# Linear attention and a gated feed-forward: kv products as half-height matmuls on alternating row halves

## The chip, the cores and the metric

The kernel runs on one core of a Trainium2 chip. A core has a matrix engine (TensorE, PE in the profile), three engines for elementwise work (VectorE or DVE, ScalarE or ACT, GpSimd or POOL), a SyncE queue that issues most transfers (SP), and 16 DMA engines. The metric is the device time of one execution in microseconds, the median of several; lower is better.

## What is computed

```python
def _attn_ref(q, k, v):                       # q, k, v: (8, 8, 576, 64), f32
    def phi(x):
        return np.where(x > 0, x, np.exp(x) - 1.0) + 1.0
    q_p, k_p = (phi(q), phi(k))
    kv = np.einsum('bhsd,bhse->bhde', k_p, v)
    z = np.sum(k_p, axis=2)
    num = np.einsum('bhsd,bhde->bhse', q_p, kv)
    den = np.einsum('bhsd,bhd->bhs', q_p, z)[..., None] + 1e-06
    return num / den

def _moe_ref(x, w1, w2, w3, w_out):           # x: (4608, 512); w1, w2: (512, 1024)
    a = x @ w1                                # w3: (1024, 1024); w_out: (1024, 512)
    b_ = x @ w2
    h = a * b_ @ w3
    return h @ w_out
```

The attention is linear: for each of 64 batch-head pairs, kv is a 64x64 product over the sequence of 576, and z is a sum of phi(k). The result, as 4608 tokens of 512 features, goes through two projections, their product, and two more matrices. The kernel multiplies w3 by w_out once (w_f) and uses that.

## The kernel before

A token batch b has 576 = 4 x 128 + 64 positions: four full chunks ("J") and a rest of 64 ("R"). The rests of heads 0 to 3 lie on partitions 0 to 63 and those of heads 4 to 7 on partitions 64 to 127. The body is one long list of short steps in a fixed order, the string ORDER; the letter is the step, then batch (or token chunk) and part. L, M, N load k, q, v; E, C, B load the weights w3, w_out, w1 and w2; x, y, z (for k) and X, Y, Z (for q) are the exp, min and max of phi; v casts v; K makes kv; A is the numerator and denominator; T and a, b transpose q; P and D transpose the result; F is one f block of the two projections; O is one output block, S its store, Q the last one; w, U, W make w_f; c, d, e, f, g and h, i serve the first batch. A "+" after a step moves its copy from ScalarE to VectorE (or a load of a rest from SyncE's queue to GpSimd's).

The pools. A tile of at_ps is two PSUM banks, of mm_ps one:

```python
    ld = ctx.enter_context(tc.tile_pool(name="ld", bufs=5))       # raw q, k, v and w3 blocks
    lr = ctx.enter_context(tc.tile_pool(name="lr", bufs=2))
    sm = ctx.enter_context(tc.tile_pool(name="sm", bufs=3))
    mm_ps = ctx.enter_context(tc.tile_pool(name="mm_ps", bufs=4, space=bass.MemoryType.PSUM))
    at_ps = ctx.enter_context(tc.tile_pool(name="at_ps", bufs=2, space=bass.MemoryType.PSUM))
```

The kv step, K. A pair of heads (hp) makes one 128x130 product: 128 features of two heads by twice 64 values and a column of ones, which gives z. Four matmuls contract over 128 positions and one over the 64 of the rest, all into one bank. A step does two pairs, and one copy takes the result to SBUF:

```python
    def kv_full(b, g):


        kj, kr = ph["k", b]
        if g == 0:
            kvs[b] = att.tile([P, KC, 2, D + 1], BF16, tag="kv", name="kv")
        kvp = at_ps.tile([P, 2, 512], F32, tag="at", name="kvp")
        W = 2 * (D + 1)
        rows = slice(g * R, (g + 1) * R)
        for i in range(2):
            hp = 2 * g + i
            for j in range(NJ):
                nc.tensor.matmul(kvp[:, 0, i * W:(i + 1) * W],
                                 kj[:, hp, j].rearrange("p u d -> p (u d)"),
                                 vt[:, j, 2 * hp:2 * hp + 2, :].rearrange("p h e -> p (h e)"),
                                 start=(j == 0), stop=False)
            nc.tensor.matmul(kvp[:, 0, i * W:(i + 1) * W], kr[rows, i * P:(i + 1) * P],
                             vr[rows, 2 * i:2 * i + 2, :].rearrange("p h e -> p (h e)"),
                             start=False, stop=True)
        return kvp[:, 0, 0:2 * W]

    def kv_copy(b, g, p, alt=False):
        copy_of(alt)(out=kvs[b][:, 2 * g:2 * g + 2].rearrange("p a u e -> p (a u e)"), in_=p)
```

The step A, which reads kv. Each matmul contracts over the 64 features of one head, so it uses one row half of the array (u = 0 or 1) and writes the bank of that half; a full chunk has stationary tiles of 64x128, the rest of 64x64:

```python
            ... (cut)
            nd = at_ps.tile([P, 2, 512], F32, tag="at", name="nd")
            if j == 0:
                xns[b] = att.tile([P, NJ, H, D], BF16, tag="xn", name="xn")
            if j < NJ:
                n, dst = P, xns[b][:, j]
            else:
                n = R
                dst = xns[b, "R"] = att.tile([R, H, D], BF16, tag="xnr", name="xnr")
            for hp in range(KC):
                if j < NJ:
                    w = qts[b, 0][:, hp, j * P:(j + 1) * P]
                else:
                    hh, i = divmod(hp, 2)
                    w = qts[b, 1][:, i, hh * R:(hh + 1) * R]
                for u in range(2):
                    rows = slice(u * D, (u + 1) * D)
                    nc.tensor.matmul(nd[0:n, u, hp * (D + 1):(hp + 1) * (D + 1)], w[rows],
                                     kvs[b][rows, hp, u, :], start=True, stop=True)
            v4 = nd[0:n, :, 0:KC * (D + 1)].rearrange("p u (c e) -> p u c e", e=D + 1)
            r = lr.tile([P, 2, KC], F32, tag="r", name="r", bufs=4)
            work.append((n, dst, v4, r))
        for n, dst, v4, r in work:
            nc.vector.tensor_scalar_add(out=r[0:n], in0=v4[:, :, :, D], scalar1=1e-6)
        for n, dst, v4, r in work:
            nc.vector.reciprocal(out=r[0:n], in_=r[0:n])
        for n, dst, v4, r in work:
            nc.vector.tensor_tensor(
                out=dst.rearrange("p (c u) e -> p u c e", u=2), in0=v4[:, :, :, 0:D],
                in1=r[0:n].unsqueeze(3).to_broadcast([n, 2, KC, D]), op=ALU.mult)
```

The step F (two times four matmuls of 512 columns, a ScalarE copy and a VectorE product) and the step O (eight matmuls of 512 columns and a copy):

```python
    def f_open(c, f):
        if f == 0:
            abs_[c] = ab_p.tile([P, FC, NCH], BF16, tag="ab", name="ab")
        return [mm_ps.tile([P, NCH], F32, tag="mm", name=n) for n in ("a_ps", "b_ps")]

    def f_mm(c, f, ps, w, kc):
        nc.tensor.matmul(ps, w[:, kc, f * P:(f + 1) * P], xt[:, 4 * c:4 * c + 4, kc, :],
                         start=(kc == 0), stop=(kc == KC - 1))

    def f_close(c, f, a_ps, b_ps):
        a_sb = sm.tile([P, NCH], F32, tag="a_sb", name="a_sb")
        nc.scalar.copy(out=a_sb, in_=a_ps)
        nc.vector.tensor_mul(out=abs_[c][:, f, :], in0=a_sb, in1=b_ps)

    def f_unit(c, f):
        a_ps, b_ps = f_open(c, f)
        for ps, w in ((a_ps, w1_sb), (b_ps, w2_sb)):
            for kc in range(KC):
                f_mm(c, f, ps, w, kc)
        f_close(c, f, a_ps, b_ps)

    def o_unit(c, m, alt=False):
        ab = abs_[c]
        o_ps = mm_ps.tile([P, DM], F32, tag="mm", name="o_ps")
        for f in range(FC):
            nc.tensor.matmul(o_ps, ab[:, f, m * P:(m + 1) * P], wf_sb[:, f, :],
                             start=(f == 0), stop=(f == FC - 1))
        o_sb = o_sbs[c, m] = sm.tile([P, DM], F32, tag="o_sb", name="o_sb", bufs=OBUF)
        copy_of(alt)(out=o_sb, in_=o_ps)
```

The w3 blocks share the pool ld with q, k and v; four blocks make one tile, and each block is transposed on TensorE:

```python
    def load_w3(i):
        if i % 4 == 0:
            t = ld.tile([P, JW], F32, tag="ld", name="w3b")
            w3s[i // 4] = t.bitcast(BF16).rearrange("p (i n) -> p i n", i=4)
        t = raw["w3", i] = w3s[i // 4][:, i % 4]
        return nc.gpsimd.dma_start(out=t, in_=moe_w3[i * P:(i + 1) * P, :])

    def w3_tr(i, alt=False):
        t = w3ts[i] = setup.tile([P, FC, P], BF16, tag="w3t", name="w3t", bufs=3)
        tp = at_ps.tile([P, FC, P], BF16, tag="at", name="w3p")
        for kc in range(FC):
            nc.tensor.transpose(tp[:, kc, :], raw["w3", i][:, kc * P:(kc + 1) * P], ident)
        copy_of(alt)(out=t, in_=tp)
```

Of the kernel before, what the change touches and what calls it, by code (L numbers as in the profile page):

```python
# [18 lines left out]
def kernel(  # L19
# [11 lines left out]
    nc = tc.nc  # L31
    B, H, S, D = q.shape
# [28 lines left out]
    att = ctx.enter_context(tc.tile_pool(name="att", bufs=2))  # L61
    lr = ctx.enter_context(tc.tile_pool(name="lr", bufs=2))
# [3 lines left out]
    at_ps = ctx.enter_context(tc.tile_pool(name="at_ps", bufs=2, space=bass.MemoryType.PSUM))  # L66
# [12 lines left out]
    vt = wpool.tile([P, NJ, H, D + 1], BF16)  # L79
    vr = wpool.tile([P, H // 2, D + 1], BF16)  # L80
# [44 lines left out]
    ph = {}  # L125
# [39 lines left out]
    def copy_of(alt):  # L165
        return nc.vector.tensor_copy if alt else nc.scalar.copy
# [309 lines left out]
    GATES = "E4<M0.1 L0.0<E0 L1.2<E3 M0.0<E0 M1.2<C1 N1.0<E7"
    ctx.enter_context(tc.manual_schedule())
# [13 lines left out]
    def step(s):  # L491

        alt = s.endswith("+")
        op, *at = s.rstrip("+").replace(".", " ").split()
        b = int(op[1:]) if op[1:] else None
        i = int(at[0]) if at else None
        t = op[0]
        if t == "F":
            f_unit(b, i)
        elif t == "O":  # L500
            o_unit(b, i, alt)
        elif t == "S":
            o_store(b, i)
        elif t == "Q":
            o_last(b, i)
        elif t == "I":
            constants(b)
        elif t == "H":
            warm_up(b)
        elif t == "w":  # L510
            w3_tr(b, alt)
        elif t == "U":
            wf_mm(b, 0)
            held["U", b] = True
# [87 lines left out]
```

## Time and profile before

| | |
|---|---|
| median of 3 runs | 264.65 us (264.34 to 265.21) |
| span of the profiled run | 263.7 us |
| matmuls, weight loads | 1544, 1561 in the records (some matmul records are missing) |
| TensorE clock granted | 1.0 throughout |
| HBM | 38.80 MB read, 9.44 MB written |

The page gives busy time per engine; "PEld" is the loading of stationary operands, which overlaps the matmuls. Digits in the rows of slices are tenths of a slice (1/40 of the span, 6.6 us). A line of the waits reads: engine and source line, the engine and line that released it, total us, number of times, longest. In the lists of instructions, 128*128 or 64*128 after a matmul is rows*columns of its stationary operand, and 128x130 is partitions x columns of the moving one. Times of matmuls overlap, as they are pipelined, so the distance between starts tells what one costs.

By group (total busy us, mean ns of one): the F matmuls 75.1 and 74.9 (380, 379), the O matmuls 63.2 (379), kv full height 12.7 (222), kv rest 7.3 (227), A 5.9 and 2.2 (192, 197). The copy of kv is ten times on ScalarE (3.7 us, 374 ns) and four times on VectorE (1.7 us, 427 ns).

### The profile page before, as it was taken

The page shows a single profiled execution, that of the slowest core. Times are in us where ns is not written, and L with a number is a line of the kernel's source. Part 1 is how long each engine was busy: PE and PEld are TensorE (multiplying, and loading weights), DVE is VectorE, ACT ScalarE, POOL GpSimd, SP SyncE. Part 2 cuts the span into 40 slices and gives each one's busy share as a digit, 9 for nine tenths or more (in the row PEclk, how much of TensorE's full clock was granted, in tenths as well). Part 3 has the DMA queues.
Part 4 walks back from the last instruction along what each step waited for, and adds up shares of the span by engine and source line. Part 5 has one row for each costly group of instructions (what it writes and reads, how often), then busy time and mean ns, then how long its engine had stood idle before and what let it go on. Part 6 is the DMA issues. An engine that isn't in the chain of part 4 may idle for free.

```text
span 263.7 us, 4270 instructions
## 1 busy us (share of the span) xinstructions
PE 241.5 (92%) x1544; PEld 118.5 (45%) x1561; DVE 167.9 (64%) x421; ACT 125.0 (47%) x196; POOL 20.1 (8%) x40
## 2 busy tenths in 40 slices
PE   1149999899999999999999999999999999999993
PEld 1125454445454455455444444454445444444442
DVE  0037688769976978999867389557974744324330
ACT  1048576856858663677244454545432212331411
POOL 8001754000100001000000000000000000000000
PEclk9999999999999999999999999999999999999999
DMA  6999999999798398959959996923871063002024
GB/s 88 215 257 368 311 231 235 221 339 283 266 300 226 43 318 221 311 137 266 217 112 245 265 286 124 277 70 108 233 199 42 9 136 106 0 22 98 2 80 160
DMA packets 70564, 48.97 MB, mean 186 GB/s; under 512 B 34928, under 2 KB 64880, under 8 KB 70544
## 3 DMA queue, kind: packets, MB, share of 16 engines
q1 hardware_dynamic: 63648, 42.67, 59.4%
q0 software_dynamic: 6752, 5.90, 13.7%
q8 instruction: 12, 0.20, 0.3%
q10 hardware_dynamic: 144, 0.13, 0.1%
q14 instruction: 8, 0.07, 0.1%
HBM read 38.80 MB, written 9.44 MB: 183 GB/s over the span
## 4 chain that ended last, share of the span: by engine, by line
PE 81%; DMA 13%; SPq 2%; ACT 1%; issue 1%; DVE 0%; POOL 0%; POOLq 0%
PE a_ps L345 24%; PE b_ps L345 23%; PE o_ps L364 23%; DMA w3b<-in_moe_w_dram 5%; DMA k<-in_k_dram 4%; DMA v<-in_v_dram 4%; PE kvp L193 3%; PE nd L239 3%; PE kvp L197 2%; SPq L111 1%; PE wf_ps L438 1%; PE tp L283 1%; PE xtp L259 1%; PE o_ps L391 1%; PE w3p L428 1%
## 5 line engine op out<-in xcount | busy, mean ns | idle before, releaser
L345 PEld LDWEIGHTS <-w_sb 128*128 128x128 bf16 x576 | 54.2, 98 | 62.5
L351 DVE TENSOR_TENSOR ab<-a_sb,b_ps 128x512 bf16<-128x512 f32 x72 | 49.2, 685 | 51.5 <-PE b_ps L345 40.4
L345 PE MATMUL a_ps<-xt,w_sb 128*128 128x512 bf16 x288 | 75.1, 380 | 0.0
L345 PE MATMUL b_ps<-xt,w_sb 128*128 128x512 bf16 x288 | 74.9, 379 | 0.0
L350 ACT COPY a_sb<-a_ps 128x512 f32<-128x512 f32 x72 | 42.0, 585 | 60.9 <-PE a_ps L345 59.8
L364 PE MATMUL o_ps<-wf_sb,ab 128*128 128x512 bf16 x266 | 63.2, 379 | 0.7
L364 PEld LDWEIGHTS <-ab 128*128 128x128 bf16 x280 | 26.7, 98 | 30.8 <-DVE ab L351 0.2
L367 ACT COPY o_sb<-o_ps 128x512 f32<-128x512 f32 x21 | 12.2, 583 | 35.0 <-PE o_ps L364 35.0
L162 DVE SCALAR_TENSOR_TENSOR kj<-k,e 128x256 bf16<-128x256 f32 x64 | 23.7, 417 | 0.1
L162 DVE SCALAR_TENSOR_TENSOR qj<-q,e 128x256 bf16<-128x256 f32 x64 | 23.4, 417 | 0.2
L137 ACT ACTIVATE e<-q 128x1024 bf16<-128x1024 f32 x16 | 16.7, 1058 | 13.2 <-DMA q<-in_q_dram 13.0
L428 PE MATMUL w3p<-ident,w3b 128*128 128x128 bf16 x64 | 6.2, 253 | 15.8 <-DMA w3b<-in_moe_w_dram 8.0
L137 ACT ACTIVATE e<-k 128x1024 bf16<-128x1024 f32 x16 | 16.9, 1055 | 3.8 <-DMA k<-in_k_dram 2.4
L249 DVE TENSOR_TENSOR xn<-nd,r 128x512 bf16<-128x512 f32 x28 | 18.0, 686 | 0.0
L438 PE MATMUL wf_ps<-wo_sb,w3t 128*128 128x512 bf16 x61 | 16.8, 414 | 0.7 <-ACT w3t L429 0.5
L367 DVE COPY o_sb<-o_ps 128x512 f32<-128x512 f32 x14 | 9.6, 688 | 10.6 <-PE o_ps L364 10.6
L141 DVE TENSOR_SCALAR er<-er 128x256 bf16<-128x256 bf16 x16 | 3.5, 220 | 17.4 <-ACT er L137 17.4
L141 DVE TENSOR_SCALAR e<-e 128x1024 bf16<-128x1024 bf16 x32 | 13.5, 421 | 0.3 <-ACT e L137 0.3
L193 PE MATMUL kvp<-vt,kj 128*128 128x130 bf16 x128 | 12.7, 222 | 0.9 <-ACT vt L171 0.9
L428 PEld LDWEIGHTS <-w3b 128*128 128x128 bf16 x64 | 4.9, 114 | 17.5 <-DMA w3b<-in_moe_w_dram 9.3
L193 PEld LDWEIGHTS <-kj 128*128 128x128 bf16 x128 | 8.3, 98 | 5.3 <-issue 1.3
L171 ACT CAST vt<-v 128x1024 bf16<-128x1024 f32 x9 | 9.4, 1046 | 0.9 <-DMA v<-in_v_dram 0.9
(77 smaller groups left out, 155.7 us busy)
## 6 DMA issues: line engine op xcount, KB each, us to landing
out_dram<-o_sb SPq DMA_DIRECT2D x31, 256.0 KB, 3.2
k<-in_k_dram SPq DMA_DIRECT2D x7, 1024.0 KB, 8.0
q<-in_q_dram SPq DMA_DIRECT2D x7, 1024.0 KB, 7.4
v<-in_v_dram SPq DMA_DIRECT2D x6, 1024.0 KB, 5.9
w3b<-in_moe_w_dram POOLq DMA_DIRECT2D x8, 256.0 KB, 7.6
v<-in_v_dram SPq DMA_DIRECT2D x4, 512.0 KB, 9.1
w_sb<-in_moe_w_dram POOLq DMA_DIRECT2D x8, 256.0 KB, 11.5
out_dram<-o_sb SPq DMA_DIRECT2D x9, 128.0 KB, 2.5
```

The lines of the kernel that those rows point to most:

```text
L137: nc.scalar.activation(out=e, in_=x, func=AF.Exp)
L141: nc.vector.tensor_scalar_min(out=e, in0=e, scalar1=1.0)
L162: nc.vector.scalar_tensor_tensor(out=out, in0=x, scalar=1.0, in1=e, op0=ALU.add, op1=ALU.max)
L193: nc.tensor.matmul(kvp[:, 0, i * W:(i + 1) * W], kj[:, hp, j].rearrange("p u d -> p (u d)"), vt[:, j, 2 * hp:2 * hp + 2, :].rearrange("p h ...
L249: nc.vector.tensor_tensor(out=dst.rearrange("p (c u) e -> p u c e", u=2), in0=v4[:, :, :, 0:D], in1=r[0:n].unsqueeze(3).to_broadcast([n, 2 ...
L345: nc.tensor.matmul(ps, w[:, kc, f * P:(f + 1) * P], xt[:, 4 * c:4 * c + 4, kc, :], start=(kc == 0), stop=(kc == KC - 1))
L350: nc.scalar.copy(out=a_sb, in_=a_ps)
L351: nc.vector.tensor_mul(out=abs_[c][:, f, :], in0=a_sb, in1=b_ps)
L364: nc.tensor.matmul(o_ps, ab[:, f, m * P:(m + 1) * P], wf_sb[:, f, :], start=(f == 0), stop=(f == FC - 1))
L367: copy_of(alt)(out=o_sb, in_=o_ps)
L428: nc.tensor.transpose(tp[:, kc, :], raw["w3", i][:, kc * P:(kc + 1) * P], ident)
L438: nc.tensor.matmul(wfs[i], w3ts[i][:, kc, :], wo_sb[:, kc, :], start=(kc == 0), stop=(kc == FC - 1))
```

## The change

All 14 K steps of batches 1 to 7 become half-height: a new step splits each 128-row contraction into two of 64 rows, issued alternately to row half 0 and row half 1 of the array. Each half accumulates in a bank of its own (kvp[:, 0] and kvp[:, 1]), so the two sums are added at the end: ScalarE copies one to SBUF, VectorE adds the other. The first batch (step c) stays as it was. The "+" of K now selects the new step. The aim is that TensorE stays in one row mode within a K step, in place of changing at each rest. The order of all steps was searched anew with a model that charges each change of row mode; the diff of ORDER is cut to the rows that the text speaks of.

```diff
--- before.py
+++ after.py
@@ -178,8 +178,34 @@
 
     kvs, qts, xns = {}, {}, {}
 
+    def kv_half(b, g):
+
+
+        kj, kr = ph["k", b]
+        if g == 0:
+            kvs[b] = att.tile([P, KC, 2, D + 1], BF16, tag="kv", name="kv")
+        kvp = at_ps.tile([P, 2, 512], F32, tag="at", name="kvp")
+        W = 2 * (D + 1)
+        for i in range(2):
+            hp = 2 * g + i
+            steps = [(kj[:, hp, j].rearrange("p u d -> p (u d)"),
+                      vt[:, j, 2 * hp:2 * hp + 2, :].rearrange("p h e -> p (h e)"), (0, 1))
+                     for j in range(NJ)]
+            steps.append((kr[:, i * P:(i + 1) * P],
+                          vr[:, 2 * i:2 * i + 2, :].rearrange("p h e -> p (h e)"), (g,)))
+            for n, (kk, vv, halves) in enumerate(steps):
+                for r in halves:
+                    rows = slice(r * R, (r + 1) * R)
+                    nc.tensor.matmul(
+                        kvp[:, r, i * W:(i + 1) * W], kk[rows], vv[rows],
+                        start=(n == 0), stop=(n == (NJ if r == g else NJ - 1)))
+        kvf = lr.tile([P, 2 * W], F32, tag="kvf", name="kvf")
+        nc.scalar.copy(out=kvf, in_=kvp[:, 0, 0:2 * W])
+        nc.vector.tensor_tensor(
+            out=kvs[b][:, 2 * g:2 * g + 2].rearrange("p a u e -> p (a u e)"), in0=kvf,
+            in1=kvp[:, 1, 0:2 * W], op=ALU.add)
+
     def kv_full(b, g):
-
 
         kj, kr = ph["k", b]
         if g == 0:
@@ -442,36 +468,36 @@
 
 
     ORDER = """
-    L0.3 E0 I0 M0.0 N0.3 E1 X0.0 w0 E2 x0.2 M1.3 w1 y0.2 L0.0 x0.0 Y0.0 M0.1 N0.0 X1.2 X0.1 C0
-    w2 Z0.0 C1 U0 Z0.1 W0+ L0.1 y0.0 N1.3 z0.4 N0.1 z0.0 a0.0 I1 Y0.1 Z0.2 Z0.3 E3 U1 v0.0+ b0.0
-    I2 U2 x0.1 w3 v0.2 W1+ a0.1 W2 v0.1+ H9 z0.1 L1.2 E4 y0.1 b0.1 c0.0 z0.2 E5 L1.3+ U3 d0.0
     ... (cut)
-    M0.3 W7+ e0.3 X1.0 Y1.0 N2.3 f0.3 h0.0 B3 h0.1 z1.3 M2.2 Z1.0 v1.0 L2.3 z1.4 Z1.1 X1.1 h0.2
-    K1.0 g0.3 Y1.1 h0.3 v1.1 a1.0 Z1.2 Z1.4 L2.2 i0.0 K1.1+ b1.0 Z1.3 i0.1 F0.2 a1.1 b1.1 X2.2
     ... (cut)
-    F1.2 F1.3 N3.3+ y3.2 K2.0 T0.1 K2.1 F1.4 X3.0 A2.0 x3.0 M4.2 F1.5 z3.4 X3.1 N3.2 y3.0 r0
     ... (cut)
-    F2.1 z4.4 K3.0+ Y4.2 F2.2 K3.1 Z4.0 Z4.1 S0.3 Z4.2 F2.3 A3.0 x4.0 Z4.3 Z4.4 v4.0 L5.2 L5.3
-    F2.4 F2.5 A3.1 y4.0 F2.6 x4.1 P3.1 z4.0 z4.1 F2.7 A2.2 P3.2 v4.1+ P3.0 O2.2 M5.2 M5.3 x5.0
     ... (cut)
-    K4.0 x5.1 Y5.0 K4.1 Z5.0 z5.0 O2.3 N5.2 Z5.1 Y5.2 A4.0 F3.3 v5.0+ S1.0 y5.1 F3.4 A4.1 S1.3
     ... (cut)
-    z5.1 x6.0 Y6.2 O3.1+ O3.3 D4.0 y6.0 z5.2 z5.3 z5.4 T5.1 F4.0 x6.2 M6.2 A4.2 T5.0 K5.0 F4.1
-    F4.2 K5.1 Z6.4 X6.0 F4.3 S2.3 X6.1 A5.0 F4.4 z6.0 L7.2 F4.5 Y6.0 S3.1 y6.2 L7.3 F4.6 A5.1
     ... (cut)
-    T7.0 K7.0+ F6.3 K7.1 F6.4 A7.0 F6.5 F6.6 S5.0 A7.1 F6.7 D7.0 O6.2 A7.2 O5.3+ O6.0+ O6.3+
     ... (cut)
-    F8.3 S6.1 S7.3 S6.3 O7.2 F8.4 F8.5 F8.6 F8.7 O8.3+ O8.0 O8.1+ S7.0 S8.3 S8.0 O7.1 S8.1 S7.2
     ... (cut)
+    L0.3 E0 I0 M0.0 x0.2 N0.3 E1 X0.0 w0 y0.2 M1.3 E2 w1 L0.0 x0.0 Y0.0 M0.1 N0.0 X1.2 X0.1 C0
+    w2 Z0.0 C1 U0 Z0.1 W0 L0.1 y0.0 N1.3 z0.4 N0.1 a0.0 I1 Y0.1 Z0.2 Z0.3 E3 z0.0 U1 I2 U2 v0.0+
+    b0.0 x0.1 w3 v0.2 W1+ a0.1 W2 v0.1+ H9 z0.1 L1.2 E4 y0.1 b0.1 c0.0 z0.2 E5 L1.3+ U3 d0.0
     ... (cut)
+    N1.1 M0.3 e0.3 X1.0 Y1.0 h0.0 f0.3 N2.3 B3 z1.3 h0.1 M2.2 Z1.0 Z1.1 v1.0 L2.3+ z1.4 X1.1
+    h0.2 g0.3 K1.0+ Y1.1 Z1.2 h0.3 Z1.4 v1.1 a1.0 L2.2 i0.0 K1.1+ b1.0 Z1.3 i0.1 F0.2 a1.1 b1.1
     ... (cut)
+    v2.0 b2.1+ F1.2 F1.3 K2.0+ T0.1 K2.1+ y3.2 F1.4 X3.0 A2.0 x3.0 M4.2 F1.5 z3.4 X3.1 y3.0 r0
     ... (cut)
+    F2.1 N5.3+ z4.4 K3.0+ S0.3 Z4.0 Y4.2 F2.2 K3.1+ Z4.1 Z4.2 F2.3 Z4.3 Z4.4 A3.0 x4.0 v4.0 L5.2
+    L5.3 F2.4 F2.5 A3.1 y4.0 F2.6 z4.0 z4.1 x4.1 P3.1 F2.7 A2.2 P3.2 v4.1+ P3.0 O2.2 M5.2 M5.3
     ... (cut)
+    S2.2 K4.0+ x5.1 Y5.0 K4.1+ Z5.0 y5.1 z5.0 O2.3 N5.2 Z5.1 S1.0 Y5.2 A4.0 F3.3 S1.3 v5.0+ F3.4
     ... (cut)
+    S1.1 z5.1 x6.0 Y6.2 O3.3 y6.0 D4.0 z5.2 z5.3 T5.0 z5.4 O3.1+ T5.1 F4.0 A4.2 x6.2 M6.2 K5.0+
+    F4.1 F4.2 K5.1+ Z6.4 X6.0 F4.3 S2.3 X6.1 A5.0 F4.4 z6.0 L7.2 Y6.0 F4.5 M7.3 N6.2 S3.1 y6.2
     ... (cut)
+    v7.1 z7.2 D6.0 Z7.1 v7.2 z7.3 O5.1 Z7.2 v7.0 O5.2+ Z7.3 D6.1 O5.0 S4.1 S5.2 F6.0 S5.1 T7.0
+    F6.1 F6.2 K7.0+ K7.1+ F6.3 F6.4 A7.0 F6.5 F6.6 S5.0 A7.1 F6.7 O6.2 O5.3+ O6.0+ A7.2 O6.3+
     ... (cut)
+    O7.0+ S7.3 F8.3 S6.1 S6.3 O7.2 F8.4 F8.5 F8.6 F8.7 O8.3+ O8.0 O8.1 S7.0 S8.3 S8.0 O7.1 S8.1
     ... (cut)
@@ -536,7 +562,10 @@
         elif t == "T":
             qt_load(b, i)
         elif t == "K":
-            kv_copy(b, i, kv_full(b, i), alt)
+            if alt:
+                kv_half(b, i)
+            else:
+                kv_copy(b, i, kv_full(b, i))
         elif t == "A":
             nat_units(b, ((0, 1), (2, 3), (4,))[i])
         elif t == "D":
```

More of the change, by code (lines that the diff above doesn't have):

```diff
@@ L444 @@
     ORDER = """
-    L0.3 E0 I0 M0.0 N0.3 E1 X0.0 w0 E2 x0.2 M1.3 w1 y0.2 L0.0 x0.0 Y0.0 M0.1 N0.0 X1.2 X0.1 C0
-    w2 Z0.0 C1 U0 Z0.1 W0+ L0.1 y0.0 N1.3 z0.4 N0.1 z0.0 a0.0 I1 Y0.1 Z0.2 Z0.3 E3 U1 v0.0+ b0.0
-    I2 U2 x0.1 w3 v0.2 W1+ a0.1 W2 v0.1+ H9 z0.1 L1.2 E4 y0.1 b0.1 c0.0 z0.2 E5 L1.3+ U3 d0.0
-    e0.0 z0.3 E6 w4+ M1.2 E7 f0.0 B0 x1.0 W3+ c0.1 w5 g0.0 d0.1 y1.0 U4 x1.2 z1.0 x1.1 W4+ e0.1
-    f0.1 w6+ e0.2 v1.2+ f0.2 Y1.2 g0.1 W5+ M2.3+ z1.1 N1.0 w7 B1 y1.2 g0.2 y1.1 B2 W6 z1.2 N1.1
@@ L450 @@
-    M0.3 W7+ e0.3 X1.0 Y1.0 N2.3 f0.3 h0.0 B3 h0.1 z1.3 M2.2 Z1.0 v1.0 L2.3 z1.4 Z1.1 X1.1 h0.2
-    K1.0 g0.3 Y1.1 h0.3 v1.1 a1.0 Z1.2 Z1.4 L2.2 i0.0 K1.1+ b1.0 Z1.3 i0.1 F0.2 a1.1 b1.1 X2.2
-    T1.1 F0.3 A1.0 X0.2 F0.4 F0.5 Y2.2 A1.1 P1.1 X2.0 P1.0+ Y2.0 F0.6 Z2.4 F0.7 Z2.0 X2.1 P1.2
-    O0.1 L3.3 x2.0 Y2.1 Y0.2 Z2.1 P1.3+ Z2.2 O0.0 y2.0 Z2.3 z2.0 x2.2 z2.1 v2.2 N2.2 x2.1 O0.2
-    Z0.4 a2.0 b2.0+ y2.1 A1.2 z2.2 M3.2 y2.2 v2.1 F1.0 F1.1 x3.2 L3.2 z2.3 a2.1 v2.0 b2.1+ z2.4
-    F1.2 F1.3 N3.3+ y3.2 K2.0 T0.1 K2.1 F1.4 X3.0 A2.0 x3.0 M4.2 F1.5 z3.4 X3.1 N3.2 y3.0 r0
@@ L456 @@
-    z3.0 D1.1 Y3.0 F1.6 L4.3 M4.3 O0.3 Y3.1 A2.1 F1.7 z3.1 S0.0 N4.3 Z3.0 S0.1 M3.3+ M6.3 X3.2
-    X4.2 S0.2 X4.0 Z3.1 Z3.2 Y3.2 X4.1 Z3.3 O1.2 D2.0 Z3.4 O1.3+ a3.0 x4.2 O1.0+ Y4.1 y4.2 v3.2+
-    N4.2 L4.2 a3.1 N6.3 v3.0+ x3.1 y3.1 v3.1+ b3.0 O1.1 b3.1 F2.0 z3.2 z3.3 N5.3 T2.1 T3.1 Y4.0
-    F2.1 z4.4 K3.0+ Y4.2 F2.2 K3.1 Z4.0 Z4.1 S0.3 Z4.2 F2.3 A3.0 x4.0 Z4.3 Z4.4 v4.0 L5.2 L5.3
-    F2.4 F2.5 A3.1 y4.0 F2.6 x4.1 P3.1 z4.0 z4.1 F2.7 A2.2 P3.2 v4.1+ P3.0 O2.2 M5.2 M5.3 x5.0
-    y4.1 T4.0 P3.3+ X5.2 A3.2 x5.2 F3.0 z4.2 X5.0 z4.3 v4.2+ S1.2 y5.2 S2.2 X5.1 F3.1 y5.0 F3.2
@@ L462 @@
-    K4.0 x5.1 Y5.0 K4.1 Z5.0 z5.0 O2.3 N5.2 Z5.1 Y5.2 A4.0 F3.3 v5.0+ S1.0 y5.1 F3.4 A4.1 S1.3
-    D3.1 Z5.4 D2.1 L6.3+ O2.0 Y5.1 v5.2 L6.2 Z5.2 F3.5 Z5.3 F3.6 v5.1+ O2.1 X6.2 F3.7 T4.1 S1.1
-    z5.1 x6.0 Y6.2 O3.1+ O3.3 D4.0 y6.0 z5.2 z5.3 z5.4 T5.1 F4.0 x6.2 M6.2 A4.2 T5.0 K5.0 F4.1
-    F4.2 K5.1 Z6.4 X6.0 F4.3 S2.3 X6.1 A5.0 F4.4 z6.0 L7.2 F4.5 Y6.0 S3.1 y6.2 L7.3 F4.6 A5.1
-    z6.1 Z6.0 D4.1 M7.3 N6.2 Z6.1 Y6.1 S2.1 x6.1 N7.3 F4.7 x7.0 z6.4 x7.1 S3.3 A5.2 S2.0 O3.2
-    y6.1 O4.0+ D5.0 O3.0 M7.2 O4.3 X7.2 Z6.2 z6.2 S3.2 v6.2 x7.2 Z6.3 O4.2+ S4.0 v6.0 F5.0 T6.0
@@ L468 @@
-    y7.0 z6.3 y7.1 F5.1 K6.0 v6.1 Y7.2 F5.2 F5.3 K6.1+ O4.1 S3.0 X7.0 z7.0 X7.1 Z7.4 T6.1 A6.0
-    y7.2 F5.4 A6.1 Y7.1 F5.5 F5.6 z7.1 F5.7 D5.1 T7.1 Y7.0 N7.2 z7.4 A6.2 S4.2 Z7.0 v7.1 z7.2
-    O5.2+ D6.0 S4.3 Z7.1 v7.2 z7.3 O5.1+ Z7.2 v7.0 D6.1 O5.0 S4.1 Z7.3 S5.2 F6.0 S5.1 F6.1 F6.2
-    T7.0 K7.0+ F6.3 K7.1 F6.4 A7.0 F6.5 F6.6 S5.0 A7.1 F6.7 D7.0 O6.2 A7.2 O5.3+ O6.0+ O6.3+
-    F7.0 F7.1 O6.1+ D7.1 F7.2 F7.3 F7.4 F7.5 F7.6 S6.0 S6.2 F7.7 F8.0 O7.3 F8.1 S5.3 F8.2 O7.0+
-    F8.3 S6.1 S7.3 S6.3 O7.2 F8.4 F8.5 F8.6 F8.7 O8.3+ O8.0 O8.1+ S7.0 S8.3 S8.0 O7.1 S8.1 S7.2
@@ L474 @@
-    S7.1 Q8.2
+    L0.3 E0 I0 M0.0 x0.2 N0.3 E1 X0.0 w0 y0.2 M1.3 E2 w1 L0.0 x0.0 Y0.0 M0.1 N0.0 X1.2 X0.1 C0
+    w2 Z0.0 C1 U0 Z0.1 W0 L0.1 y0.0 N1.3 z0.4 N0.1 a0.0 I1 Y0.1 Z0.2 Z0.3 E3 z0.0 U1 I2 U2 v0.0+
+    b0.0 x0.1 w3 v0.2 W1+ a0.1 W2 v0.1+ H9 z0.1 L1.2 E4 y0.1 b0.1 c0.0 z0.2 E5 L1.3+ U3 d0.0
+    e0.0 z0.3 E6 w4+ M1.2 E7 f0.0 B0 x1.0 W3+ c0.1 w5 g0.0 U4 d0.1 y1.0 x1.2 z1.0 W4+ x1.1 e0.1
+    f0.1 w6+ e0.2 v1.2+ g0.1 Y1.2 f0.2 W5 M2.3+ w7 N1.0 g0.2 B1 y1.2 y1.1 z1.1 B2 W6 z1.2 W7+
+    N1.1 M0.3 e0.3 X1.0 Y1.0 h0.0 f0.3 N2.3 B3 z1.3 h0.1 M2.2 Z1.0 Z1.1 v1.0 L2.3+ z1.4 X1.1
@@ new lines @@
+    h0.2 g0.3 K1.0+ Y1.1 Z1.2 h0.3 Z1.4 v1.1 a1.0 L2.2 i0.0 K1.1+ b1.0 Z1.3 i0.1 F0.2 a1.1 b1.1
+    X2.2 T1.1 F0.3 A1.0 F0.4 F0.5 Y2.2 X0.2 A1.1 P1.1 X2.0 P1.0+ Y2.0 F0.6 Z2.4 Z2.0 X2.1 F0.7
+    P1.2 x2.0 O0.1 Y2.1 Y0.2 Z2.1 P1.3+ L3.3 Z2.2 O0.0 y2.0 Z2.3 N3.3+ z2.0 x2.2 z2.1 v2.2 N2.2
+    O0.2+ x2.1 Z0.4 a2.0 b2.0+ y2.1 A1.2 z2.2 M3.2 y2.2 F1.0 L3.2 z2.4 F1.1 x3.2 v2.1 z2.3 a2.1
+    v2.0 b2.1+ F1.2 F1.3 K2.0+ T0.1 K2.1+ y3.2 F1.4 X3.0 A2.0 x3.0 M4.2 F1.5 z3.4 X3.1 y3.0 r0
+    z3.0 D1.1 Y3.0 F1.6 L4.3 N3.2 M4.3 O0.3 Y3.1 A2.1 F1.7 z3.1 S0.0 N4.3 S0.1 Z3.0 M3.3+ M6.3
@@ new lines @@
+    X3.2 S0.2 X4.2 X4.0 Z3.1 Z3.2 X4.1 Y3.2 Z3.3 O1.2 D2.0 Z3.4 O1.3+ a3.0 x4.2 O1.0+ Y4.1 y4.2
+    v3.2+ N4.2 L4.2 a3.1 N6.3 v3.0+ x3.1 v3.1+ y3.1 b3.0 O1.1 b3.1 F2.0 z3.2 z3.3 T2.1 T3.1 Y4.0
+    F2.1 N5.3+ z4.4 K3.0+ S0.3 Z4.0 Y4.2 F2.2 K3.1+ Z4.1 Z4.2 F2.3 Z4.3 Z4.4 A3.0 x4.0 v4.0 L5.2
+    L5.3 F2.4 F2.5 A3.1 y4.0 F2.6 z4.0 z4.1 x4.1 P3.1 F2.7 A2.2 P3.2 v4.1+ P3.0 O2.2 M5.2 M5.3
+    x5.0 y4.1 T4.0 P3.3+ X5.2 A3.2 x5.2 S1.2 z4.2 F3.0 X5.0 z4.3 v4.2+ y5.2 X5.1 F3.1 y5.0 F3.2
+    S2.2 K4.0+ x5.1 Y5.0 K4.1+ Z5.0 y5.1 z5.0 O2.3 N5.2 Z5.1 S1.0 Y5.2 A4.0 F3.3 S1.3 v5.0+ F3.4
@@ new lines @@
+    A4.1 D3.1 Z5.4 D2.1 L6.3 O2.0 Y5.1 v5.2 L6.2 F3.5 Z5.2 Z5.3 F3.6 v5.1+ O2.1 X6.2 F3.7 T4.1
+    S1.1 z5.1 x6.0 Y6.2 O3.3 y6.0 D4.0 z5.2 z5.3 T5.0 z5.4 O3.1+ T5.1 F4.0 A4.2 x6.2 M6.2 K5.0+
+    F4.1 F4.2 K5.1+ Z6.4 X6.0 F4.3 S2.3 X6.1 A5.0 F4.4 z6.0 L7.2 Y6.0 F4.5 M7.3 N6.2 S3.1 y6.2
+    L7.3 F4.6 A5.1 z6.1 Z6.0 D4.1 Z6.1 Y6.1 x6.1 N7.3 S2.1 F4.7 x7.0 x7.1 S3.3 z6.4 A5.2 S2.0
+    O3.2 y6.1 O4.0+ D5.0 O4.3 X7.2 Z6.2 z6.2 S3.2 v6.2 x7.2 Z6.3 y7.1 O4.2 M7.2 S4.0 O3.0 v6.0
+    F5.0 T6.0 y7.0 z6.3 v6.1 F5.1 K6.0+ Y7.2 F5.2 F5.3 K6.1+ O4.1 S3.0 X7.0 z7.0 Z7.4 X7.1 T6.1
@@ L475 @@
+    A6.0 y7.2 F5.4 A6.1 Y7.1 F5.5 F5.6 z7.1 F5.7 D5.1 T7.1 Y7.0 N7.2 z7.4 A6.2 S4.2 Z7.0 S4.3
+    v7.1 z7.2 D6.0 Z7.1 v7.2 z7.3 O5.1 Z7.2 v7.0 O5.2+ Z7.3 D6.1 O5.0 S4.1 S5.2 F6.0 S5.1 T7.0
+    F6.1 F6.2 K7.0+ K7.1+ F6.3 F6.4 A7.0 F6.5 F6.6 S5.0 A7.1 F6.7 O6.2 O5.3+ O6.0+ A7.2 O6.3+
+    D7.0 F7.0 F7.1 O6.1 D7.1 F7.2 F7.3 F7.4 F7.5 F7.6 S6.0 S6.2 F7.7 F8.0 O7.3 F8.1 S5.3 F8.2
+    O7.0+ S7.3 F8.3 S6.1 S6.3 O7.2 F8.4 F8.5 F8.6 F8.7 O8.3+ O8.0 O8.1 S7.0 S8.3 S8.0 O7.1 S8.1
+    S7.2 S7.1 Q8.2
     """
```

## The prediction

> **What bounds the kernel now.** I read four views, in this order. First the page's top, for the load of each engine over time:
>
> ```profile
> PE 241.5 (92%) x1544; PEld 118.5 (45%) x1561; DVE 167.9 (64%) x421; ACT 125.0 (47%) x196; POOL 20.1 (8%) x40
> PE   1149999899999999999999999999999999999993
> DVE  0037688769976978999867389557974744324330
> DMA  6999999999798398959959996923871063002024
> ```
>
> TensorE is at nine tenths or more from the eleventh slice to the last but one, while DMA is full only in the first third. A busy row need not be a limiting one, so next the waits, asked for TensorE alone:
>
> ```profile
> PE w3p L428 <- DMA w3b<-in_moe_w_dram: 8.0, 4, 5.1
> PE w3p L428 <- ACT w3t L429: 7.9, 1, 7.9
> PE kvp L193 <- ACT vt L171: 0.9, 2, 0.6
> PE wf_ps L438 <- ACT w3t L429: 0.5, 1, 0.5
> ```
>
> The list is complete: 17.3 us, all of it in the opening, the last wait being that of K1.1 (kv of batch 1, second half) at 50.48 us for its cast v. After that TensorE never waits for another engine. This can be tested by adding up the matmuls of the order list from K1.1 on, at start-to-start distances measured in the trace (216 ns for 512 columns, 109 for 256, 57 for 130, 56 for 128, 32 for a pair of nd matmuls): 70 F and 35 O units of eight, 181.4 us; the last output 1.7; transposes 4.0; 13 K units at 0.57, 7.4; 21 A units, 4.5; the batch-0 rest 0.2. That makes 199.3. The remaining term is what this change is about. The timeline of TensorE around one K unit:
>
> ```profile
> 100.42 0.39 PE L193 MATMUL kvp<-vt,kj 128*128 128x130 bf16 x4
> 100.74 0.23 PE L197 MATMUL kvp<-vr,kr 64*128 64x130 bf16 x1
> 100.90 0.40 PE L193 MATMUL kvp<-vt,kj 128*128 128x130 bf16 x4
> 101.24 0.23 PE L197 MATMUL kvp<-vr,kr 64*128 64x130 bf16 x1
> 101.40 0.39 PE L345 MATMUL a_ps<-xt,w_sb 128*128 128x512 bf16 x1
> ```
>
> Columns: start, time, then rows*columns of the stationary operand. Four full-height matmuls begin 57 ns apart, but the 64-row one comes 152 ns after the fourth, and the next 128-row one 160 ns after it. A step into 64 rows thus costs 152 - 57 = 95 ns and a step out 160 - 57 = 103 ns. It is the same elsewhere: 311 instead of 216 ns from an F matmul into an nd unit. Ten matmuls at 57 plus four changes (396 ns) make 0.97 us, and the timeline has 0.98. From K1.1 on there are 13 x 4 changes in K units and 21 x 2 in A units, 94 in all, near 0.1 us each: 9.3 us. 199.3 + 9.3 = 208.6 us, and the trace has 209.0 from 50.48 to the last output matmul's end, less its drain. So every change of row mode is paid in full in the kernel's time, and nothing else hides behind it.
>
> **What the Trainium skill says.** "TensorEngine Tiling (Array Packing)", Key Properties: changing the tiling mode, not just the tile, drains TensorE. The 95 and 103 ns above agree. The same page, Gotcha 1: PSUM Pressure, says that different row tiles must write different banks; the new unit does (bank r for row half r). "TensorE: Matmul & The Clock Gate", Part 3, says that matmuls on different row groups run concurrently, starting about 4 ns apart. The A units here are just this case: u = 0 and u = 1 lie on the two row halves, and in the unit at 105.94 us their starts are 3 to 5 ns apart, with the next pair some 32 ns later; sixteen of them plus the exit take the 0.36 us to 106.30. "Advanced Engine Details and Errata", Engine Queue Depths, gives TensorE 64 places. In that unit 32 instructions, weight loads included, go through in 0.24 us, so issue did not limit.
>
> **The change part by part.**
>
> *TensorE.* In all 14 K units of batches 1 to 7 the marker "+" now means half height: 18 matmuls (8 of row half 0, 8 of half 1, two rests on half g) instead of 8 full and 2 rests. 112 more matmuls, but they alternate halves. The half with the rests has 10 to run and the other 8, so a unit takes 10 x 57 = 0.57 us if the two halves overlap as in A: no more and no less streaming than before. What goes is changes: per unit two (one in, one out) remain of four. In 14 units, 14 x (95 + 103) = 2.77 us. The rest comes from neighbours. K2.0/K2.1 and K4.0/K4.1 were already adjacent and K7.0/K7.1 are made so; each pair stays in 64-row mode between its units, 3 x 2 changes more, 0.59 us. And K5.0 follows A4.2 directly: one change instead of two, 0.1 us, if 64x64 to 64x128 counts as one. From K1.0 on, 98 changes become 63; sum 3.5 us. The remaining sequence of TensorE is the old one but for some O units swapped, so nothing is added.
>
> *ScalarE and VectorE.* A K unit was emptied by one copy (ten on ScalarE at 374 ns, four on VectorE at 427). Now each needs a ScalarE copy of one half and a VectorE add of the other. I take 0.43 us for the add, from the kvz row (128x256, PSUM input, 420 ns). VectorE: 14 x 0.43 - 4 x 0.427 = +4.3; ScalarE: 4 x 0.374 = +1.5. The new order also moves three o copies and two wf casts from VectorE to ScalarE: -3.4 and +2.9. Net VectorE +0.9, ScalarE +4.4. Neither lies on the path by its sum (64% and 47% busy).
>
> *Latency.* kv is ready later by one VectorE add and a handover, some 0.5 us, while its reader A comes earlier by the changes saved. The tightest place is batch 4: after K4.1 only one O unit (1.73 us) stands before A4.0. Before, ScalarE ran copy, a 1.06 us exp, copy, done at 124.85, and A4.0 began at 125.97: 1.1 us to spare. Afterwards A4.0 would begin near 125.3 and the second copy end near 124.7, the add near 125.15: some 0.15 us to spare. Batch 2 has about 0.6. I charge 0.3 us for small waits in all.
>
> *Opening.* Here the instruction order of the two builds differs in one thing that matters. The second batch of w3 loads was held until TensorE had transposed the fourth block (18.9 us of wait on POOL, issue at 25.48); in the new build it takes over q's buffer and waits for the last phi step on it, which the new VectorE order brings to about 24.6. These loads gate batch 1's v, whose landing ends the chain of the opening. DMA is full at that time, so only part of the 0.8 us will arrive: -0.3 us. K1.1 still waits for v, so K1.0's share of the saving (0.2 us, already counted) may be eaten there.
>
> Sum: 264.65 - 3.5 - 0.3 + 0.3 = 261.2 us.
>
> **Rivals.**
>
> *The halves do not overlap.* Then 18 x 57 = 1.03 us of streaming a unit, +0.46 x 14 = +6.4, less the 3.5: about 267.5. For it: the kv stream has twice the columns of nd, and accumulates. Against: nd pairs overlap, on the same 64x128 tile shape with two banks, and accumulating full-height matmuls hold 57 ns. I give it 6 in 100, an incomplete overlap (pairs at 65 to 70 ns, +1 to +2 us) some 10.
>
> *VectorE becomes the bound for a stretch.* The table by stages:
>
> ```profile
> 50.00:100.00 50.00, 49.37 (x354) 24.92 (x357) 39.61 (x106) 33.45 (x55) 1.23 (x2) 1.00 0.91 253
> 100.00:120.00 20.00, 19.95 (x156) 9.97 (x156) 18.66 (x52) 11.89 (x20) 1.23 (x2) 1.00 0.84 214
> 120.00:160.00 40.00, 39.84 (x273) 18.89 (x276) 30.43 (x81) 19.03 (x33) 0.00 (x0) 1.00 0.91 225
> ```
>
> (After the length, busy us of PE, PEld, DVE, ACT.) From 100 to 120 us VectorE is busy 18.66 of 20. One more add (K3.1) and a shorter TensorE stretch leave about 0.6 us of air. F's multiply frees the PSUM buffer that the unit after next needs for its b half; at F2.4 it ends 0.17 us before that unit starts its a half, so about 1.0 before b. If the adds push it past this, TensorE waits, at most the overhang of 1 to 2 us: 262.5 to 263. Against: the new order puts phi steps of that stretch into an earlier gap of VectorE (Z4.0 ahead of F2.2). One in six.
>
> *The opening swallows more.* If the earlier w3 loads and the moved copies make v land later, the end shifts with it, one for one; a load order that behaves 1 us worse gives 262.2, one that behaves 1 us better 260.2.
>
> **Range and chances.** The main term is a count times a very even measured cost, so the uncertainty is in the opening (about 0.7 us either way) and in new waits, which go one way. Range 260.2 to 263.2 us. 2% is 5.3 us, 259.4 or 269.9: the first needs nearly two more us than the changes can give, the second a failed overlap and waits besides. Faster by over 2%: 0.05; within 2%: 0.92; slower by over 2%: 0.03.
>
> **What would show it.** Each step has its place in the changed profile. In a K unit: pair starts 57 ns apart and 0.77 us from its entry gap to the end of its exit gap, with kvp matmuls at 64*128 only. From K1.0 to the end TensorE some 3.5 us shorter. TensorE's waits: still nothing beyond the opening, or new entries such as PE nd on DVE kv (latency) or PE b_ps on DVE ab (VectorE). The start of K1.1 near 50.2. I would be wrong if kvp starts ran singly at 57 ns, if TensorE's wait list held more than 1 us after the opening, or if K1.1 began more than 1 us from 50.5.

## The result, and the profile after

The changed kernel takes 260.71 us (median of 3 runs, 260.10 to 261.39) against 264.65 (264.34 to 265.21): ratio 0.985, 95% interval 0.980 to 0.990. Beside the experiments it was measured again (4 runs, and 19 of the kernel before): 260.42 us against 265.32, ratio 0.983 (0.981 to 0.985). Of the 1.0 us between the two differences, 0.7 is the kernel before. The prediction was 261.2 us, range 260.2 to 263.2.

The top of the page after (busy us and share, then tenths in 40 slices):

```profile
PE 237.4 (92%) x1656; PEld 116.2 (45%) x1673; DVE 167.9 (65%) x426; ACT 129.0 (50%) x205; POOL 21.1 (8%) x42
PE   1138999999999999999999999999999999999994
```

There are 112 more matmuls, and TensorE is still busy to the end: 237.4 us in place of 241.5. VectorE did not change in sum (predicted +0.9), ScalarE got 4.0 us more (predicted 4.4). All waits of TensorE after:

```profile
PE w3p L454 <- ACT w3t L455: 8.0, 1, 8.0
PE w3p L454 <- DMA w3b<-in_moe_w_dram: 7.0, 3, 5.1
PE wf_ps L464 <- ACT w3t L455: 0.8, 1, 0.8
```

All lie in the opening. No nd waits for kv, no b_ps for ab. The timeline of TensorE around the K unit that the prediction showed (K3.0; start, time, rows*columns of the stationary operand):

```profile
97.89 0.40 PE L199 MATMUL kvp<-vt,kj 64*128 64x130 bf16 x8
98.13 0.22 PE L199 MATMUL kvp<-vr,kr 64*128 64x130 bf16 x1
98.13 0.44 PE L199 MATMUL kvp<-vt,kj 64*128 64x130 bf16 x8
98.41 0.22 PE L199 MATMUL kvp<-vr,kr 64*128 64x130 bf16 x1
98.56 0.39 PE L371 MATMUL a_ps<-xt,w_sb 128*128 128x512 bf16 x1
```

The first product's eight matmuls of 64 rows and its rest have started within 0.24 us: the starts come in pairs 3 to 5 ns apart, one pair every 57 ns (the second after 67). From the first start to the next F it is 0.67 us, plus 95 ns of gap ahead of it (312 ns behind an F matmul instead of 216): 0.77 us, before 0.98.

Cut at two marks, the start of K1.1 and the start of the last matmul, the traces of the two kernels compare so:

| us | before | after |
|---|---|---|
| opening, to K1.1 | 50.48 | 48.89 |
| body, K1.1 to the last matmul | 208.90 | 205.21 |
| tail, to the end of the span | 4.34 | 3.97 |

The profiled run of before took 265.98 us, 1.3 above its median, so the difference of the openings is not to be read as the kernel's.

### The profile page after: what moved, and what is told of

Same layout as the page of the kernel before. It is cut to its first block, busy times and chain, and to the rows that moved or that the text cites. A ratio compares the mean times of both kernels' runs of the same rounds, so it can differ in the third digit from the quotient of the medians.

```text
span 258.1 us, 4507 instructions
## 1 busy us (share of the span) xinstructions
PE 237.4 (92%) x1656; PEld 116.2 (45%) x1673; DVE 167.9 (65%) x426; ACT 129.0 (50%) x205; POOL 21.1 (8%) x42
## 4 chain that ended last, share of the span: by engine, by line
PE 84%; DMA 8%; ACT 2%; SPq 1%; issue 1%; DVE 1%; DVEq 0%; POOLq 0%
PE a_ps L371 25%; PE b_ps L371 24%; PE o_ps L390 23%; DMA k<-in_k_dram 4%; DMA w3b<-in_moe_w_dram 4%; PE kvp L199 3%; PE wf_ps L464 3%; PE nd L265 3%; SPq L111 1%; PE tp L309 1%; PE w3p L454 1%; PE xtp L285 1%; PE o_ps L417 1%; DVE qj L162 1%; ACT e L137 0%
## 5 line engine op out<-in xcount | busy, mean ns | idle before, releaser
L393 ACT COPY o_sb<-o_ps 128x512 f32<-128x512 f32 x24 | 14.0, 583 | 30.7 <-PE o_ps L390 30.7
L393 DVE COPY o_sb<-o_ps 128x512 f32<-128x512 f32 x11 | 7.6, 688 | 6.4 <-PE o_ps L390 6.4
L203 ACT COPY kvf<-kvp 128x260 f32<-128x260 f32 x14 | 5.3, 375 | 8.9 <-PE kvp L199 8.7
L464 PEld LDWEIGHTS <-w3t 128*128 128x128 bf16 x64 | 6.2, 104 | 7.8 <-issue 1.7
L199 PE MATMUL kvp<-vt,kj 64*128 64x130 bf16 x224 | 9.2, 217 | 0.0
```

What stands on the lines that cost most here:

```text
L199: nc.tensor.matmul(kvp[:, r, i * W:(i + 1) * W], kk[rows], vv[rows], start=(n == 0), stop=(n == (NJ if r == g else NJ - 1)))
L464: nc.tensor.matmul(wfs[i], w3ts[i][:, kc, :], wo_sb[:, kc, :], start=(kc == 0), stop=(kc == FC - 1))
```

## The experiments

Theory A is that of the prediction: each change of row mode on TensorE costs about 0.1 us of the end, and the kv change pays by their number. Theory B: the new order brings the gain. A further rival: what pays is that two halves stream at once. The body is given for each run, as the opening varies between profiles: K1.1 starts between 48.9 and 51.1 us.

| run | K changes in a unit on its own | ratio to before, 95% interval | body us |
|---|---|---|---|
| before | 4 | 1 | 208.90 |
| changed kernel, again | 2 | 0.983 (0.981 to 0.985) | 205.04 |
| half-height, old order | 2 | 0.988 (0.986 to 0.990) | 205.35 |
| the same, one swap | 2 | 0.989 (0.986 to 0.991) | 205.35 |
| full height, new order | 4 | 0.998 (0.997 to 0.999) | 208.90 |
| halves in blocks | 2 | 0.985 (0.983 to 0.988) | 205.84 |
| full height, rests together | 2 | 0.988 (0.986 to 0.989) | 206.18 |
| padded rest, old order | 0 | 0.979 (0.977 to 0.981) | 203.44 |
| padded rest, new order | 0 | 0.978 (0.977 to 0.980) | 203.45 |
| the same, two moves | 0 | 0.978 (0.977 to 0.980) | 203.45 |
| the same, no gate on v | 0 | 0.999 (0.996 to 1.001) | 209.35 |
| changed kernel, add twice | 2 | 0.990 (0.988 to 0.992) | 206.22 |

**Half-height in the old order.** Edit: ORDER of before, and

```diff
-            if alt:
-                kv_half(b, i)
-            else:
-                kv_copy(b, i, kv_full(b, i))
+            kv_half(b, i)
```

> Half-height kv in all 14 K steps, but the order of the kernel before. Theory A (each change of row mode costs TensorE about 0.1 us, the order matters little): ten single units save 0.21 us each, two adjacent pairs (K2, K4) 0.74 each, K5.0 behind A4.2 0.1, in all 3.7 us: 261.0 us, ratio 0.986. Theory B (the new order brings the gain, the halves only fit into it): 264.6 us, ratio 1.00. If the later kv (one VectorE add) makes A wait in an order not made for it, TensorE's waits name nd, and the ratio lies between.

Ratio 0.988, between the two theories, but not where it was looked for. The body is 205.35 us, 3.55 shorter than before: A is right there, and no nd waited. The measured time is only 3.0 us less, so some 0.5 was lost outside the body. A new wait of TensorE stands in the opening; this is it, and VectorE at that time:

```profile
PE a_ps L371 <- DVE xt L339: 1.6, 1, 1.6
```

```profile
48.08 0.42 DVE L204 TENSOR_TENSOR kv<-kvf,kvp 128x260 bf16<-128x260 f32 x1 [0.98 <-ACT kvf L203]
48.42 0.68 DVE L339 TENSOR_TENSOR xt<-nd,lr 128x512 bf16<-128x512 f32 x1
```

In the order of steps, the last product of batch 0 (g0.3) stands behind K1.0's add. The add waits 0.98 us for K1.0 and its ScalarE copy, and the product starts only as the add ends. With full height K1.0's copy was ScalarE's and nothing stood in the way. The new order has g0.3 ahead of K1.0.

**The same with that swap.**

```diff
-    K1.0 g0.3 Y1.1 h0.3 v1.1 a1.0
+    g0.3 K1.0 Y1.1 h0.3 v1.1 a1.0
```

> Half-height kv in the old order, with one swap: g0.3 (VectorE's last product of batch 0's result) ahead of K1.0, as the new order has it. In the run without the swap TensorE waited 1.6 us for that product, as it stood behind K1.0's VectorE add and so behind v. Theory A: that wait goes; 0.2 to 0.3 us (K7's adjacent pair) above the changed kernel, ratio 0.986. If the new order does more than this: the ratio stays near 0.988.

In the trace the wait for xt fell from 1.6 to 0.4 us, and K1.1's wait for its v rose from 0.2 to 0.4. The profiled run took 261.19 us, but the median is 262.00: 0.989, as without the swap. So the swap alone does not buy what the new order has; of the 1.6 us between this run and the changed kernel, the bodies explain 0.3 and the tails (4.37 and 3.96) 0.4. No profile shows the rest, and it stays open.

**The new order at full height.**

```diff
-            if alt:
-                kv_half(b, i)
-            else:
-                kv_copy(b, i, kv_full(b, i))
+            kv_copy(b, i, kv_full(b, i))
```

> The new order, but all 14 K steps at full height, each emptied by one ScalarE copy. Theory A: only the opening can differ, 264.3 us, ratio 0.999, TensorE's sequence from K1.0 on as long as before. Theory B: about 260.7, ratio 0.985.

0.998: theory B falls as the main cause. The body is 208.90 us, that of before to the hundredth. What the order brings by itself, 0.5 to 0.6 us, is outside the body.

**The halves in blocks.**

```diff
-            for n, (kk, vv, halves) in enumerate(steps):
-                for r in halves:
+            for r in (0, 1):
+                for n, (kk, vv, halves) in enumerate(steps):
+                    if r not in halves:
+                        continue
```

> The changed kernel, but each product runs all matmuls of row half 0 and then all of row half 1, in place of alternating. The row mode changes stay as few as in the changed kernel. If the count of changes is all that matters: 260.7 us, ratio 0.985. If the gain also needs the two halves to run side by side: 18 starts at 57 ns in a unit, 1.03 us in place of 0.52 to 0.57, some 7 us more: 267.8, ratio 1.012.

0.985, so the 7 us did not come. But this run doesn't show that overlap is needless, for they overlapped all the same. K3.0 in the timeline of TensorE:

```profile
98.61 0.42 PE L201 MATMUL kvp<-vt,kj 64*128 64x130 bf16 x7
98.85 0.22 PE L201 MATMUL kvp<-vr,kr 64*128 64x130 bf16 x1
98.87 0.44 PE L201 MATMUL kvp<-vt,kj 64*128 64x130 bf16 x8
```

In the program, also as built, four kj matmuls of half 0 stand ahead of the rest (kr) and four of half 1 behind it. In the trace seven kj matmuls start before the rest. The nine starts are 0, 68, 76, 124, 143, 181, 200, 238, 257 ns, the rest's at 238. They form two trains whose steps are 57 ns (67 or 68 at first): 0, 68, 124, 181, 238 is half 0 with its rest, and 76, 143, 200, 257 must be half 1. A unit takes 10 to 20 ns more than with alternation, an adjacent pair 130 more. Alternating in the program is thus not what makes the halves run side by side.

**Full height, rests together.** No half-height at all: the second product of a unit runs its rest first, so the two rests are neighbours. The line that does it:

```diff
+            steps = steps + [rest] if i == 0 else [rest] + steps
```

> The kernel before, full height, with one turn: the second product of a K unit runs its rest first, so the two rests stand side by side and a unit changes row mode twice in place of four times. No half-height matmuls, no added bank, copy or VectorE add. Theory A: 14 x 0.20 = 2.8 us less, ratio 0.9895, a unit of 975 ns becoming 777. If the gain of the change comes from the two halves running side by side, not from the mode: ratio 1.00.

```profile
98.62 0.39 PE L199 MATMUL kvp<-vt,kj 128*128 128x130 bf16 x4
98.95 0.28 PE L199 MATMUL kvp<-vr,kr 64*128 64x130 bf16 x2
99.16 0.40 PE L199 MATMUL kvp<-vt,kj 128*128 128x130 bf16 x4
99.40 0.38 PE L346 MATMUL a_ps<-xt,w_sb 128*128 128x512 bf16 x1
```

From 98.62 to 99.40 it is 777 ns, as expected. 0.988: body 206.18, 2.72 less for 26 fewer changes, 0.105 us each. Turning one loop around brings 0.70 to 0.74 of the changed kernel's gain in the body, without a second bank, a copy or an add. The rival "two streams at once" falls as the main cause: here nothing streams at once.

**The rest padded to 128 rows.** kr stays as it is, with four heads on each row half; vr gets a second copy, so that each is zero on the other row half (edit shortened).

```diff
-    vr = wpool.tile([P, H // 2, D + 1], BF16)
+    vr = wpool.tile([P, 2, H // 2, D + 1], BF16)      # zeroed once
-            copy_of(alt)(out=vr[:, :, 0:D], in_=...)
+            for x in range(2):                          # rows of half x
+                copy_of(alt)(out=vr[rows, x, :, 0:D], in_=...[rows])
-            nc.tensor.matmul(..., kr[rows, i * P:(i + 1) * P], vr[rows, 2 * i:2 * i + 2, :], ...)
+            nc.tensor.matmul(..., kr[:, i * P:(i + 1) * P], vr[:, g, 2 * i:2 * i + 2, :], ...)
```

> The kernel before with its order, full height throughout: the rest is multiplied at 128 rows too, with a vr that is zero on the other row half (two copies of 64 partitions each in place of one of 128). No row mode change is left in K. Theory A: 14 units save 4 changes, 0.40 us each, 5.5 us: 259.1 us, ratio 0.979, better than the changed kernel, with 975 ns of a unit becoming 580. If the gain of the change came from streaming two halves at once and not from the mode, this has the streaming of before and the ratio is 1.00.

```profile
98.06 0.39 PE L197 MATMUL kvp<-vt,kj 128*128 128x130 bf16 x4
98.28 0.22 PE L201 MATMUL kvp<-vr,kr 128*128 128x130 bf16 x1
98.34 0.39 PE L197 MATMUL kvp<-vt,kj 128*128 128x130 bf16 x4
98.56 0.22 PE L201 MATMUL kvp<-vr,kr 128*128 128x130 bf16 x1
98.62 0.38 PE L349 MATMUL a_ps<-xt,w_sb 128*128 128x512 bf16 x1
```

All at 128*128, ten matmuls in 567 ns. 259.88 us, 0.979: the body is 5.46 us shorter for 52 fewer changes, again 0.105 each. The two copies of vr (402 ns on ScalarE, 328 on VectorE) hide. With the new order:

> The new order with the zero-padded rest at full height in all K steps (one ScalarE copy each, no VectorE add). Theory A: the body from K1.1 on as in the kernel with the old order and padded rest (203.4 us to the last matmul), as the order does not matter there; the opening 0.3 to 0.6 us shorter as with the new order at full height: ratio 0.977 to 0.978, about 259.2 us. If the orders matter for the body: over 1 us off that.

259.63 us, 0.978 (0.977 to 0.980), the same body; the order is again worth nothing in it. This is faster than the kernel before and than the changed one (0.983).

**Two moves in the opening.** K1.0 of the changed kernel lost time to kr and to xt. The moves are made in the kernel with the padded rest and the new order.

```diff
-B3 z1.3 h0.1 M2.2 Z1.0 Z1.1 v1.0 L2.3+ z1.4 X1.1 h0.2 g0.3 K1.0+
+B3 z1.3 z1.4 h0.1 M2.2 Z1.0 g0.3 Z1.1 v1.0 L2.3+ X1.1 h0.2 K1.0+
```

> The same, with two steps moved in the opening: z1.4 (the last operand of K1.0) directly behind z1.3, and g0.3 ahead of Z1.1, both on VectorE. In the changed kernel K1.0 lost 0.28 us inside and 0.15 at its exit to these. If that is on the path: 0.4 us less than the run without the move. If v of batch 1 sets the start of K1.1 anyway: the same time, with the gain turned into a wait of K1.1 for vt.

The second case: no change (0.978). K1.0 loses nothing more inside or at its exit, and K1.1 begins 1217 instead of 974 ns after the matmul ahead of it, at 50.26 and 50.31 us. In these two runs batch 1's v sets that point; the list has K1.1 waiting 1.0 us for it.

**No gate on v.**

```diff
-    GATES = "E4<M0.1 L0.0<E0 L1.2<E3 M0.0<E0 M1.2<C1 N1.0<E7"
+    GATES = "E4<M0.1 L0.0<E0 L1.2<E3 M0.0<E0 M1.2<C1"
```

> The padded rest, new order, the two VectorE moves in the opening, and no gate that holds batch 1's v back until the last w3 block has landed: v is issued when its buffer comes free, some 5 us earlier. If v's late landing is what bounds the start of K1.1 (1.0 us of wait there): up to 1 us less, ratio 0.974 to 0.976. Rival: DMA is full then, so v takes from w3 and w1/w2, and the wait moves to w3p or to the first a_ps: ratio 0.978 or worse.

v is issued at 27.7 us in place of 38.3 (10.6 us earlier, not some 5), and K1.1 starts at 49.01, 1.25 us earlier; the end is 5.5 us later. TensorE now waits for w1 and w2 behind it:

```profile
PE b_ps L348 <- DMA w_sb<-in_moe_w_dram: 2.6, 3, 1.3
PE a_ps L348 <- DMA w_sb<-in_moe_w_dram: 1.4, 1, 1.4
```

The rival was right: what v gains, the weights lose, and more. The body is 5.9 us longer than with the gate; these waits are 4.0 of it. The windows show where the rest lies (us from and to, length, busy PE, PEld, DVE, ACT, POOL, then the clock that TensorE was granted, DMA share, GB/s):

```profile
56.00:60.00 4.00, 3.67 (x36) 1.84 (x36) 1.88 (x8) 1.37 (x3) 0.00 (x0) 1.00 1.55 232
60.00:66.00 6.00, 3.58 (x11) 1.20 (x12) 2.59 (x7) 2.61 (x4) 0.00 (x0) 0.78 1.02 262
66.00:72.00 6.00, 6.00 (x34) 2.91 (x33) 4.95 (x15) 2.96 (x5) 0.00 (x0) 0.94 0.93 331
```

The clock is down at the end of the second window and the start of the third: 6 x 0.22 + 6 x 0.06 = 1.7 us of full speed. The starts agree: behind the last wait, from 63.46 to 66.79 us, eight steps between F matmuls are 373 to 427 ns long in place of 216, 1.6 us in all.

**The add twice.**

```diff
+        for _ in range(2):
             nc.vector.tensor_tensor(out=kvs[b][...], in0=kvf, in1=kvp[:, 1, 0:2 * W], op=ALU.add)
```

> The changed kernel with its VectorE add of each K step done twice: 14 x 0.36, 5 us more for VectorE. Theory A (TensorE alone sets the body): ratio as the changed kernel, 0.985, at most 0.3 us of waits. Rival (VectorE is close to being the bound in the stretch of batches 3 and 4, where it had 1.3 us of air in 20): TensorE waits there for ab, 1 to 2 us more, ratio 0.989 to 0.993.

VectorE has 5.7 us more, as an add takes 0.42 us and not 0.36. 0.990, the body 1.0 to 1.2 us longer, as the rival had it in size. (The time rose by 2 to 3 us; 0.5 of this is a longer tail, and the rest, outside the body, is not explained.) TensorE's listed waits for VectorE in the body are these:

```profile
PE nd L266 <- DVE xn L276: 0.3, 1, 0.3
PE nd L266 <- DVE kv L205: 0.2, 1, 0.2
```

The first, at 109.83 us, is the wait of A for a PSUM tile that batch 3's product still reads; the second, at 125.47, is A4.0 for its kv. The prediction named both places. But the first is not the wait that it and the expectation named there: TensorE never waits for ab. So the changed kernel fits, but with less air than one more add per unit.

The changed kernel once more, for its interval:

> The changed kernel once more, for a narrower interval beside the others: 0.985 (261.3 us beside a kernel before of 265.3).

0.983, a little better than expected; the changed kernel is 4 to 5 us faster than before. The padded rest gains some 0.3 to 0.5% more.

## Why the prediction was right

*The main term* was right in kind and somewhat small in size. Predicted from K1.0 on: 3.5 us, so 3.3 from K1.1. Measured: 3.7 and 3.9. Three ways of removing changes give one price, 0.10 to 0.11 us each: 2.72 us for 26, 5.46 for 52, and in the changed kernel 3.35 to 3.5 for 33, once 0.34 is taken off that its adjacent pairs gain otherwise (below). Two parts of the sum were mis-sized. A single unit went from 975 to between 766 and 770 ns (0.21, not 0.20), as the way out costs 92 ns behind a pair. An adjacent pair went from 1.96 to 1.22 us, 0.74 and not 0.6. I had counted ten matmuls on the longer half for each unit. But g = 0 puts its rests on half 0 and g = 1 on half 1, so a pair has 18 on each half, not 20: 2 x 57 ns less, three times.

*K5.0 behind A4.2* counts as one change, as assumed: its first start is 126 ns behind the last of A, where the kernel before had 125 for the step out of the mode.

*The waits I charged, 0.3 us,* did not come; the rival that VectorE binds a stretch was not reached, though a doubled add shows it to be near.

*The overlap* was right. That it needs alternate issue was nowhere predicted in so many words, but one branch of the expectation for the blocks rested on it, and its 7 us did not come.

*The opening* is the step that failed. I had the second batch of w3 loads issued at 24.6 us, when VectorE's last phi step on q is done. That step ended at 24.67, but the issue came at 25.29. The waits of GpSimd name another:

```profile
POOL w3b L445 <- ACT qt L311: 18.7, 1, 18.7
```

It was released with ScalarE's copy of the transposed q, which the new order puts after another copy. In the run with the new order at full height the issue came at 26.25 and K1.1 at 50.35. v was issued between 37.4 and 38.8 us in the gated runs of either order. Nor did K1.1 still wait for v, as I had it: in the profiled run of the changed kernel it starts 151 ns behind a transpose of 128 columns, which is 56 and a step into 64 rows. My sign for a failed prediction (K1.1 over 1 us from 50.5) did appear, at 48.89. But the other gated runs have it at 49.30 to 50.56 in the old order and at 49.30 to 51.06 in the new one, so no effect of the order on the start of K1.1 is shown. The full-height run with the new order is 0.5 to 0.6 us faster than before; 0.37 of it is a shorter tail in its profile, a term that the prediction did not have. Why the tail is shorter was not tried, and two runs with the new order had a long one (4.40 and 4.47).

So 261.2 came from +0.3 that did not happen, a main term 0.4 to 0.6 too small, and -0.3 for the opening whose reason did not hold. That the first and the last cancel is luck. Against the first measurement (3.9 us less) the sum is 0.5 short. Of the 4.9 us of the second, body and tail explain 4.2; the other 0.7 stays open.

## What to carry to other kernels

Where TensorE never waits, as in this body, its own small gaps are the time: take the starts of neighbouring matmuls, subtract the streaming, and count what is left by kind. Changes of row mode can be removed in more than one way; grouping the odd ones or padding them with zeros is simpler than splitting all the others, and here padding gained most. Before moving a copy to an engine that works in order, look at what stands behind it in that engine's queue.

## What the runs showed that I had not expected

Matmuls on different row halves start out of program order. In the run with blocks, half 1's first matmul starts 76 ns after half 0's first, ahead of three that precede it in the program. "TensorE: Matmul & The Clock Gate", Part 3, says in the Trainium skill that matmuls start and end strictly in program order; these starts differ from it for two row groups, and the measurement decides. The price of a change of row mode is very even: 93 to 96 ns in and 92 to 103 out in the traces of the two kernels, and the same between 64x64 and 64x128 tiles. The traces also show what goes with it. In the unit K3.0 of the kernel before, a weight load within a mode starts 1 to 2 ns after the matmul ahead of its own; that of the rest starts 148 ns after it (100.739 against 100.591 us), 4 ns before its own matmul. So nothing is loaded ahead across a change. As such a load takes 92 to 98 ns by itself, no run here separates a load that is no longer hidden from an array that has to run empty first.
